# A fused attention and two-MLP kernel: seventeen weight units of the second MLP converted ahead, four raw buffers, and the x blocks in shared room

## The chip, the core and the metric

The kernel runs on one core of a Trainium2 chip. TensorE (PE) multiplies, VectorE (DVE), ScalarE (ACT) and GpSimd (POOL) work on what lies in SBUF and PSUM, and SyncE (SP) issues every DMA here. Each engine takes its own instructions in the order in which they stand in its queue, and waits on semaphores for the others. The metric is the device time in microseconds (us) of one execution of the whole program.

## What is computed

Attention with normalised q and k, a first MLP that is a product of two linear maps followed by two more, and a second MLP, which this change is about:

```python
def _moe2_ref(x, w_in, w_out):
    h = x @ w_in                          # 1792x768 @ 768x2048
    relu6 = np.clip(h + 3.0, 0.0, 6.0)
    g = h * relu6 / 6.0
    return (g @ w_out).astype(np.float32) # 1792x2048 @ 2048x768
```

The weights of both MLPs come in as 64-bit floats; q, k, v and all results are 32-bit.

## The kernel before

**Precision.** A product of 32-bit values is made of three matmuls (`mm3`, L80 to L83): each operand is split into a rounded part (hi) and the difference (lo), and hi·hi (L81), hi·lo (L82) and lo·hi (L83) are added up in PSUM.

**Weight units of the second MLP.** `win` and `wo2` are cut into 16 units each of 128 x 768, numbered 0 to 31: unit 2m is the part of `win` for step m, unit 2m+1 the part of `wo2` for step m. A unit goes through four stations. `load_w` (L818) brings its 64-bit words into a raw buffer `wr`, of which there are two. `conv_w` (L822) makes 32-bit floats of them with `convert` (L130): two ACT instructions (L137, L138) and two DVE instructions (L140, then L143, which writes the unit's tile `wf`). After that the raw buffer is free, and `conv_w(q)` issues the load of unit q+2 into it. `wf` stays in SBUF for the whole of the second MLP. Whenever a step uses the unit, `split` (L832) makes hi of it on ACT (L834) and lo on POOL (L835), as `wis` (from `win`) or `wos` (from `wo2`), each with two buffers.

**Steps and blocks.** The tokens are cut into four blocks of 448 columns, the block computed last by the first MLP goes first. Each block b runs through 16 steps m. Step m computes h (18 matmuls into one of two PSUM banks of tag `s`), then makes g of it: `u` on ACT (L906), `u` on DVE (L907), g hi on ACT (L910), g lo, the last difference, on DVE (L911). The second product of step m, `l4_part` (18 matmuls into six banks `acc`), is written behind h of step m+1, so TensorE has the h of the next step to do while g is made. At the end of a block the six results are copied out of `acc` (L867 to L870) and stored, and the next block's x is split into `x2h` (L810 to L813).

**What comes ahead.** The first 13 units (`NA = 13`, L797) are converted while the first MLP's last block still runs (L841 to L853), one at every third turn of the loop that also feeds the first MLP. The other units are converted in block 0: `conv_w` of units 2m+4 and 2m+5 is written at the head of step m, ahead of that step's splits (L878 to L881). The blocks of x and the results have eight tiles `xx` of 448 columns of their own (`x2tile`, L807), and x of block 1 is loaded at step 2 of block 0 (L882).

**What sets the order.** The code is written in this order, but a list scheduler places the instructions: within the data's constraints an engine's queue can differ from the written order, as the rows further down show. `tc.issue_after` keeps what is inside it behind a given instruction.

Of the kernel before, what the change touches and what calls it, by code (L numbers as in the profile page):

```python
# [12 lines left out]
F32 = mybir.dt.float32  # L13
# [4 lines left out]
AF = mybir.ActivationFunctionType  # L18
# [5 lines left out]
B, H, S, D = 4, 12, 448, 64  # L24
HP = H // 2
NP = B * HP
P = 128
# [3 lines left out]
DM = H * D  # L31
# [4 lines left out]
M2 = F2 // P  # L36
# [11 lines left out]
def fused_kernel(ctx: ExitStack, tc: tile.TileContext, nat, qT, kT, vin, gq, gk,  # L48
                 w12, w3t, wo, win, wo2, outT):
    nc = tc.nc  # L50
# [19 lines left out]
    def fetch(pool, src, n, tag, bufs=2):  # L70

        if src.dtype == F32:
            r = pool.tile([P, n], F32, tag=tag, bufs=bufs, name=tag)
            dma(r, src)
        else:
            r = pool.tile([P, n, 2], I32, tag=tag, bufs=bufs, name=tag)
            dma(r, src.bitcast(I32).rearrange("p (n t) -> p n t", t=2))
        return r

    def mm3(ps, lh, ll, rh, rl, first, last):  # L80
        nc.tensor.matmul(ps, lh, rh, start=first, stop=False)  # L81
        nc.tensor.matmul(ps, lh, rl, start=False, stop=False)  # L82
        return nc.tensor.matmul(ps, ll, rh, start=False, stop=last)  # L83

    def bank(tag, name="bank"):
        return pp.tile([P, 512], F32, tag=tag, name=name)

    def dma(out, src):
        return nc.sync.dma_start(out, src)
# [40 lines left out]
    def convert(w, r):  # L130

        hi, lo = r[:, :, 1], r[:, :, 0]
        top = r.bitcast(U16).rearrange("p n (t s) -> p n t s", s=2)[:, :, 0, 1]
        f = hi.bitcast(F32)
        nc.scalar.activation(f, f, AF.Copy, scale=2.0 ** -112)  # L137
        nc.scalar.activation(lo, top, AF.Copy, scale=2.0 ** -13, bias=2.0 ** -14 - 0.5)  # L138
        yield 0.7
        nc.vector.scalar_tensor_tensor(out=lo, in0=hi, scalar=SIGN, in1=lo,  # L140
                                       op0=ALU.bitwise_and, op1=ALU.bitwise_or)
        yield 0.9
        nc.vector.scalar_tensor_tensor(out=w, in0=hi, scalar=3, in1=lo,  # L143
                                       op0=ALU.logical_shift_left, op1=ALU.bitwise_or)
        yield 0.9
# [648 lines left out]
        attention(ap, rate)  # L794


    NA = 13  # L797
    order = [B - 1] + list(range(B - 1))
    d1 = ExitStack()
    x2p = d1.enter_context(tc.tile_pool(name="x2", bufs=1, side="left", **RW))  # L800
    wap = d1.enter_context(tc.tile_pool(name="wfa", bufs=1, side="left", **RW))
    xh = [None] * KD
    x2r = {}
    wf, wr = {}, {}
    wpools = [wap]

    def x2tile():  # L807
        return x2p.tile([P, S], F32, tag="xx", bufs=8, name="xx")

    def splitx2(n, src):  # L810
        d = x2p.tile([P, 2, S], F32R, tag="x2h", bufs=KD, name="x2h")
        nc.scalar.activation(d[:, 0, :], src, AF.Copy)
        nc.vector.tensor_sub(d[:, 1, :], src, d[:, 0, :])  # L813
        xh[n] = d
# [2 lines left out]

    def load_w(q):  # L818
        if q < 2 * M2:
            wr[q] = fetch(wap, (win, wo2)[q % 2][q // 2], DM, "wr", bufs=2)  # L820

    def conv_w(q):  # L822
        r = wr.pop(q)
        wf[q] = wpools[-1].tile([P, DM], F32, name=f"wf{q}")
        if r.dtype == F32:
            nc.gpsimd.tensor_copy(wf[q], r)
        else:
            for _ in convert(wf[q].bitcast(I32), r):
                pass
        load_w(q + 2)  # L830

    def split(q, tag, pool=None):  # L832
        t = (pool or lp).tile([P, 2, DM], F32R, tag=tag, bufs=2 if pool is None else 1, name=tag)
        nc.scalar.activation(t[:, 0, :], wf[q], AF.Copy)  # L834
        nc.gpsimd.tensor_sub(t[:, 1, :], wf[q], t[:, 0, :])  # L835
        return t

    load_w(0)
    load_w(1)
    step, q = 0, 0  # L840
    while not state["done"] or any(k >= now[0] for k in tasks):  # L841
        now[0] += 1
        fill(2.0, 3.0)
        run_tasks()
        step += 1
        if step > 2 and q < NA and step % 3 == 0:
            conv_w(q)
            q += 1
            if q == 1:
                wnext = split(0, "w0", wap)  # L850
    while q < NA:
        conv_w(q)
        q += 1  # L853
# [5 lines left out]
    lp = d1.enter_context(tc.tile_pool(name="l3", bufs=2, side="right", **RW))  # L859

    def l4_part(n, t, m, g, w, acc):
        ns = slice(n * P, n * P + P)
        return mm3(acc[n][:, :S], w[:, 0, ns], w[:, 1, ns], g[:, 0, :], g[:, 1, :], m == 0, m == M2 - 1)

    def out(n, t, acc):
        o = x2tile()
        if n % 2:  # L867
            nc.vector.tensor_copy(o, acc[n][:, :S])
        else:
            nc.scalar.activation(o, acc[n][:, :S], AF.Copy)  # L870
        dma(outT[n * P : n * P + P, t * S : t * S + S], o)

    pend = None
    for b, t in enumerate(order):
        acc = None
        for m in range(M2):
            last = b == B - 1 and m == M2 - 1
            if b == 0:  # L878
                for q in (2 * m + 4, 2 * m + 5):
                    if NA <= q < 2 * M2:  # L880
                        conv_w(q)  # L881
            if m == 2 and b < B - 1:  # L882
                for n in range(KD):
                    x2r[n] = x2tile()
                    dma(x2r[n], x2d[order[b + 1], n])
            w = wnext
            if not last:
                wnext = split(2 * ((m + 1) % M2), "wis")
            wos = split(2 * m + 1, "wos")
            ps = bank("s", "h2")  # L890
            for k in range(KD):
                ks = slice(k * P, k * P + P)
                mm3(ps[:, :S], w[:, 0, ks], w[:, 1, ks], xh[k][:, 0, :], xh[k][:, 1, :],
                    k == 0, k == KD - 1)
            if m == M2 - 1 and b < B - 1:
                for k in range(KD):
                    splitx2(k, x2r[k])
            if pend is not None and not last:
                for n in range(KD):
                    l4_part(n, *pend)  # L900
                    if m == 0:
                        out(n, pend[0], pend[4])
            if acc is None:
                acc = [bank(TAGS[1 + n // 2], "acc") for n in range(KD)]
            u = lp.tile([P, S], F32, tag="u", bufs=2, name="u")
            nc.scalar.activation(u, ps[:, :S], AF.Relu, bias=half, scale=1.0 / 6.0)  # L906
            nc.vector.scalar_tensor_tensor(out=u, in0=u, scalar=1.0, in1=ps[:, :S],  # L907
                                           op0=ALU.min, op1=ALU.mult)
            g = lp.tile([P, 2, S], F32R, tag="g", bufs=2, name="g")
            nc.scalar.activation(g[:, 0, :], u, AF.Copy)  # L910
            nc.vector.tensor_sub(g[:, 1, :], u, g[:, 0, :])  # L911
            before, pend = pend, (t, m, g, wos, acc)
    mm = None
    for e in (before, pend):
# [52 lines left out]
```

## Time and profile before

| | us |
|---|---|
| median of 3 runs | 1238.3 (1236.92 to 1243.6) |
| the profiled execution, its own time | 1239.83 |
| its span, first to last instruction | 1238.1 |
| PE busy | 1168.1 (94%) |
| DVE busy | 751.1 (61%) |
| ACT busy | 727.8 (59%) |
| POOL busy | 463.9 (37%) |

Attention and most of the first MLP take the first 640 us or so. The first MLP's last block and the first conversions of second-MLP weights fill the stretch to 748 us, where its last matmul runs. Block 0 of the second MLP runs from there to about 886 us, and blocks 1 to 3 take 118.4 us each, up to a short tail. A TensorE that counts as busy isn't at its peak: its matmuls are pipelined, a matmul of 448 columns counts as about 0.37 us, and a new one starts about every 0.205 us in the undisturbed blocks. So the count of matmuls in a stretch tells more of it than the busy share.

### The profile page before, as it was taken

Reading aid. Unit: us, or ns where it says so; the run is one execution under the profiler, and the core shown is the slowest. Engines: PE = TensorE matmul, PEld = TensorE weight load, DVE = VectorE, ACT = ScalarE, POOL = GpSimd, SP = SyncE. Lnnn points to the kernel's source line nnn. Section 1 sums busy time; section 2 is a strip of 40 time slices with the busy share of each in tenths; the row PEclk is TensorE's granted clock in tenths of the full one; section 3 lists DMA queues with packets and bytes.
Section 4 is the critical chain, followed back from the end, with each engine's and each line's share of the span. In section 5 each row is a group of like instructions: output and inputs, shape, how many; then the busy total and the mean of one; then the engine's idle time right before and its main releaser. Section 6 shows DMA issues by size and latency. Waiting matters only on the chain.

```text
span 1238.1 us, 16937 instructions
## 1 busy us (share of the span) xinstructions
PE 1168.1 (94%) x5868; PEld 1024.0 (83%) x5868; DVE 751.1 (61%) x1474; ACT 727.8 (59%) x1401; POOL 463.9 (37%) x316
## 2 busy tenths in 40 slices
PE   3698998988899999999999999989999999999998
PEld 2457877777789999889998998779999999999997
DVE  6977988998767787667624436774433333343332
ACT  6887788888857677666534435664533443343332
POOL 3534234553522213221020005445545445455442
PEclk9798998998999999999999999999999999999999
DMA  7667666797987777764469963440200020001001
GB/s 277 204 215 237 193 184 205 247 291 260 307 299 239 224 238 224 244 224 174 145 253 410 342 236 127 154 153 1 89 1 1 1 90 1 1 1 45 1 1 45
DMA packets 64694, 203.73 MB, mean 165 GB/s; under 512 B 8544, under 2 KB 25440, under 8 KB 64608
## 3 DMA queue, kind: packets, MB, share of 16 engines
q1 hardware_dynamic: 64608, 202.65, 48.4%
q8 instruction: 46, 0.75, 0.2%
q14 instruction: 40, 0.33, 0.1%
HBM read 173.93 MB, written 28.68 MB: 164 GB/s over the span
## 4 chain that ended last, share of the span: by engine, by line
PE 62%; DMA 4%; DVE 4%; ACT 3%; issue 2%; POOL 0%; SPq 0%; ACTq 0%; POOLq 0%; DVEq 0%
PE bank L81 7%; PE bank L83 7%; PE bank L82 7%; PE acc L81 6%; PE acc L82 6%; PE acc L83 6%; PE h L81 5%; PE h L82 5%; PE h L83 5%; PE bank L587 2%; PE bank L561 1%; PE bank L562 1%; DVE wf L143 1%; PE bank L639 1%; PE bank L640 1%
## 5 line engine op out<-in xcount | busy, mean ns | idle before, releaser
L835 POOL TENSOR_TENSOR wis<-wf,wis 128x768 fp32r<-128x768 f32 x63 | 120.9, 1919 | 234.3 <-ACT wis L834 234.3
L907 DVE SCALAR_TENSOR_TENSOR u<-u,h 128x448 f32<-128x448 f32 x64 | 39.6, 619 | 212.3 <-ACT u L906 212.3
L835 POOL TENSOR_TENSOR wos<-wf,wos 128x768 fp32r<-128x768 f32 x64 | 119.0, 1860 | 98.1 <-ACT wos L834 98.1
L580 ACT ACTIVATE PP<-PP,mx 112x448 f32<-112x448 f32 x192 | 127.4, 665 | 38.9 <-DVE mx L575 34.3
L568 DVE CUSTOM_DVE_ANT_0 PP<-bank,rb,rq 112x448 f32<-112x448 f32 x192 | 129.3, 677 | 32.0 <-PE bank L562 25.2
L81 PE MATMUL bank<-xhl,ws 128*128 128x448 f32 x384 | 143.1, 373 | 3.7 <-ACT ws L287 2.2
L83 PE MATMUL bank<-xhl,ws 128*128 128x448 f32 x384 | 141.5, 369 | 3.7 <-POOL ws L289 3.7
L82 PE MATMUL acc<-g,wos 128*128 128x448 f32 x384 | 142.6, 371 | 2.3 <-DVE g L911 2.3
L83 PE MATMUL acc<-g,wos 128*128 128x448 f32 x384 | 141.9, 369 | 0.0
L82 PE MATMUL bank<-xhl,ws 128*128 128x448 f32 x384 | 141.2, 368 | 0.0
L81 PE MATMUL acc<-g,wos 128*128 128x448 f32 x384 | 138.8, 374 | 2.5 <-ACT g L910 2.5
L81 PE MATMUL h<-x2h,wis 128*128 128x448 f32 x378 | 139.2, 368 | 0.6 <-DVE u L907 0.6
L83 PE MATMUL h<-x2h,wis 128*128 128x448 f32 x378 | 137.7, 364 | 2.2 <-POOL wis L835 2.2
L82 PE MATMUL h<-x2h,wis 128*128 128x448 f32 x378 | 139.0, 368 | 0.0
L906 ACT ACTIVATE u<-h,half 128x448 f32<-128x448 f32 x64 | 40.6, 634 | 141.1 <-PE h L83 141.1
L911 DVE TENSOR_TENSOR g<-u,g 128x448 fp32r<-128x448 f32 x64 | 99.5, 1554 | 35.4 <-ACT g L910 35.4
L606 DVE TENSOR_TENSOR xl<-bank,xh 128x448 fp32r<-128x448 f32 x142 | 87.4, 617 | 30.0 <-ACT xh L596 28.3
L834 ACT ACTIVATE wos<-wf 128x768 fp32r<-128x768 f32 x64 | 54.0, 844 | 84.2 <-PE acc L83 84.0
L587 PEld LDWEIGHTS bank<-ident,PP 112*128 112x128 f32 x672 | 79.3, 143 | 28.0 <-issue 9.7
L596 ACT ACTIVATE xh<-bank 128x448 fp32r<-128x448 f32 (+1 forms) x156 | 83.1, 539 | 32.4 <-PE bank L587 30.8
L587 PE MATMUL bank<-ident,PP 112*128 112x112 f32 x672 | 96.0, 266 | 6.5 <-DVE xl L606 5.2
L561 PE MATMUL bank<-K,Q 128*112 128x448 f32 x192 | 77.1, 403 | 24.1 <-DVE mx L568 12.7
(128 smaller groups left out, 2755.7 us busy)
## 6 DMA issues: line engine op xcount, KB each, us to landing
ws<-w12d SPq DMA_DIRECT2D x48, 768.0 KB
ws<-wpd SPq DMA_DIRECT2D x32, 768.0 KB
raw<-in_w_dram SPq DMA_DIRECT2D x32, 384.0 KB
w12d<-ws SPq DMA_DIRECT2D x16, 768.0 KB
wr<-in_win_dram SPq DMA_DIRECT2D x16, 768.0 KB
wr<-in_wo_dram SPq DMA_DIRECT2D x16, 768.0 KB
qr<-in_qT_dram SPq DMA_DIRECT2D x24, 448.0 KB
kr<-in_kT_dram SPq DMA_DIRECT2D x24, 448.0 KB
```

What stands on the lines that cost most here:

```text
L81: nc.tensor.matmul(ps, lh, rh, start=first, stop=False)
L82: nc.tensor.matmul(ps, lh, rl, start=False, stop=False)
L83: return nc.tensor.matmul(ps, ll, rh, start=False, stop=last)
L561: nc.tensor.matmul(ps[:CP, :S], qs, k1[:, j, :], start=True, stop=False)
L568: anchors[8 * i + s].append(nc.vector.tensor_tensor_reduce(out=T["PP", i][:, c, sl], in0=ps[:CP, :S], in1=T["rb", i][:, sl], op0=ALU.mult, ...
L580: anchors[8 * i + s].append(nc.scalar.activation(v, v, AF.Exp, bias=T["m", i][:, 8 + s : 9 + s], accum_out=T["sum", i][:, s : s + 1]))
L587: nc.tensor.transpose(ps[:, c * CP : c * CP + CP], src[:, c, kb * P : kb * P + P], ident[:CP, :CP])
L596: nc.scalar.activation(hi, ps, AF.Copy)
L606: nc.vector.tensor_sub(lo, ps, hi)
L834: nc.scalar.activation(t[:, 0, :], wf[q], AF.Copy)
L835: nc.gpsimd.tensor_sub(t[:, 1, :], wf[q], t[:, 0, :])
L911: nc.vector.tensor_sub(g[:, 1, :], u, g[:, 0, :])
```

## The change

`NA` goes from 13 to 17. The eight tiles `xx` are gone: `x2tile` now takes a tile of the size of a raw weight buffer (tag `wr`, two buffers, or tag `w0`, one buffer, which also holds the split unit of step 0) and hands out three parts of 448 columns of it. Four raw buffers serve the units from 17 on: the two `wr`, one more `wr` in the pool `lp` on the other side of SBUF, and `w0` after step 0; `conv_w(q)` loads unit q+4 into the one that it frees. In block 0 the conversions of step m are kept behind both last instructions of the step before (`done`: g hi and g lo), and there are one or two of them: units up to 17 + (5m+5)//4 are done after step m. The x of block 1 is loaded at step 14 instead of step 2 (m == M2 - 2); later blocks keep step 2.

```diff
-    NA = 13
+    NA = 17
...
+    xx = [0, None]
+
     def x2tile():
-        return x2p.tile([P, S], F32, tag="xx", bufs=8, name="xx")
+
+        n = 2 * DM // S if win.dtype != F32 else DM // S
+        z = xx[0] % n
+        if z == 0:
+            tag, bufs = ("w0", 1) if xx[0] // n % 3 == 2 else ("wr", 2)
+            xx[1] = wap.tile([P, n * S + (2 * DM % S if n > 1 else DM % S)], F32, tag=tag, bufs=bufs, name=tag)
+        xx[0] += 1
+        return xx[1][:, z * S : z * S + S]
...
         if q < 2 * M2:
-            wr[q] = fetch(wap, (win, wo2)[q % 2][q // 2], DM, "wr", bufs=2)
+            pool, tag, n = (wap, "wr", 2)
+            if q >= NA + 2 and (q - NA) % 4 > 1:
+                pool, tag, n = (lp, "wr", 1) if (q - NA) % 4 == 2 else (wap, "w0", 1)
+            wr[q] = fetch(pool, (win, wo2)[q % 2][q // 2], DM, tag, bufs=n)
...
-        load_w(q + 2)
+        load_w(q + (2 if q < NA else 4))
...
-    pend = None
+    load_w(NA + 2)
+
+    pend, done = None, []
...
             if b == 0:
-                for q in (2 * m + 4, 2 * m + 5):
-                    if NA <= q < 2 * M2:
+                if m == 1:
+                    load_w(NA + 3)
+                with ExitStack() as es:
+                    for i in done:
+                        es.enter_context(tc.issue_after(i.ins))
+                    while q < min(2 * M2, max(NA + (5 * m + 5) // 4, 2 * m + 6)):
                         conv_w(q)
-            if m == 2 and b < B - 1:
+                        q += 1
+            if m == (2 if b else M2 - 2) and b < B - 1:
...
-            nc.scalar.activation(g[:, 0, :], u, AF.Copy)
-            nc.vector.tensor_sub(g[:, 1, :], u, g[:, 0, :])
+            done = [nc.scalar.activation(g[:, 0, :], u, AF.Copy),
+                    nc.vector.tensor_sub(g[:, 1, :], u, g[:, 0, :])]
```

How the queues move is shown at three places. In the rows, L137, L138, L140 and L143 are the four instructions of a conversion, `wfN` is unit N, and the lines of the changed code are 12 to 19 higher (L846 is the split's L834, L925 the `u` on ACT, L926 the `u` on DVE, L929 and L930 the two halves of g, L821 the split of x).

ACT in block 0, steps 3 and 4, before:

```order
L906 ACTIVATE u_8082<-h2_8045,half_75 128x448
L834 ACTIVATE wis_8095<-wf10_7760 128x768
L137 ACTIVATE wr_8275<-wr_8275 128x768
L138 ACTIVATE wr_8275<-wr_8275 128x768
L910 ACTIVATE g_8085<-u_8082 128x448
L834 ACTIVATE wos_8098<-wf9_7714 128x768
L137 ACTIVATE wr_8282<-wr_8282 128x768
L138 ACTIVATE wr_8282<-wr_8282 128x768
L906 ACTIVATE u_8138<-h2_8101,half_75 128x448
L834 ACTIVATE wis_8158<-wf12_7853 128x768
```

The same steps, now:

```order
L925 ACTIVATE u_8137<-h2_8100,half_75 128x448
L846 ACTIVATE wis_8150<-wf10_7760 128x768
L929 ACTIVATE g_8140<-u_8137 128x448
L137 ACTIVATE wr_7973<-wr_7973 128x768
L138 ACTIVATE wr_7973<-wr_7973 128x768
L846 ACTIVATE wos_8153<-wf9_7714 128x768
L925 ACTIVATE u_8193<-h2_8156,half_75 128x448
L846 ACTIVATE wis_8206<-wf12_7853 128x768
```

Before, a conversion stood between `u` and g and another in front of the next `u`; now one stands behind g, and `u`, the split and g follow each other.

DVE at the same steps, before:

```order
L907 SCALAR_TENSOR_TENSOR u_8082<-u_8082,h2_8045 128x448
L143 SCALAR_TENSOR_TENSOR wf19_8277<-wr_8219 128x768
L140 SCALAR_TENSOR_TENSOR wr_8275<-wr_8275 128x768
L911 TENSOR_TENSOR g_8085<-u_8082,g_8085 128x448
L143 SCALAR_TENSOR_TENSOR wf20_8333<-wr_8275 128x768
L140 SCALAR_TENSOR_TENSOR wr_8282<-wr_8282 128x768
L907 SCALAR_TENSOR_TENSOR u_8138<-u_8138,h2_8101 128x448
```

The same steps, now:

```order
L926 SCALAR_TENSOR_TENSOR u_8137<-u_8137,h2_8100 128x448
L930 TENSOR_TENSOR g_8140<-u_8137,g_8140 128x448
L140 SCALAR_TENSOR_TENSOR wr_7973<-wr_7973 128x768
L143 SCALAR_TENSOR_TENSOR wf22_8143<-wr_7973 128x768
L926 SCALAR_TENSOR_TENSOR u_8193<-u_8193,h2_8156 128x448
```

Here too the halves of conversions that stood between `u` and g, and ahead of the next `u`, have become one conversion behind g; it is of unit 22 where it was of 19 to 21.

ACT at the end of the first MLP, from the split of x's third or fourth part (of six) to the first splits of weights, before:

```order
L137 ACTIVATE wr_7858<-wr_7858 128x768
L138 ACTIVATE wr_7858<-wr_7858 128x768
L812 ACTIVATE x2h_7837<-bank_7783 128x448
L812 ACTIVATE x2h_7869<-bank_7818 128x448
L812 ACTIVATE x2h_7881<-bank_7846 128x448
L834 ACTIVATE wis_7892<-wf2_7370 128x768
L834 ACTIVATE wos_7895<-wf1_7320 128x768
```

The same place, now:

```order
L821 ACTIVATE x2h_7837<-bank_7783 128x448
L137 ACTIVATE wr_7858<-wr_7858 128x768
L138 ACTIVATE wr_7858<-wr_7858 128x768
L137 ACTIVATE wr_7889<-wr_7889 128x768
L138 ACTIVATE wr_7889<-wr_7889 128x768
L821 ACTIVATE x2h_7869<-bank_7818 128x448
L137 ACTIVATE wr_7896<-wr_7896 128x768
L138 ACTIVATE wr_7896<-wr_7896 128x768
L821 ACTIVATE x2h_7881<-bank_7846 128x448
L846 ACTIVATE wis_7929<-wf2_7370 128x768
L846 ACTIVATE wos_7932<-wf1_7320 128x768
```

Unit 14 (`wr_7858`) has moved behind x's fourth part, and the conversions of units 15 and 16 stand ahead of its fifth and sixth. Unit 17's stands behind four splits of weights and ahead of block 0's first `u`. So 18 conversions now stand ahead of that `u` on ACT, where there were 15.

## Rows read from the trace of the kernel before

**Rows 1.** Windows: start:end, length, busy us (count) by engine, TensorE clock, DMA share, GB/s.

```profile
748.00:886.60 138.60, 130.99 (x608) 115.25 (x607) 88.19 (x78) 79.34 (x114) 71.69 (x36) 0.98 0.30 105
886.60:1005.00 118.40, 118.40 (x577) 108.09 (x576) 43.60 (x41) 48.54 (x73) 59.16 (x32) 1.00 0.07 23
...
787.00:794.00 7.00, 5.49 (x18) 4.07 (x17) 6.56 (x6) 4.56 (x7) 4.03 (x3) 0.76 0.44 150
...
822.00:829.00 7.00, 5.20 (x17) 4.43 (x17) 4.39 (x5) 4.87 (x7) 3.69 (x2) 0.76 0.56 209
```

**Rows 2.** Waits of PE, 748 to 886.6 us: us in total, times, longest.

```profile
PE acc L81 <- ACT g L910: 2.5, 3, 1.3
PE acc L82 <- DVE g L911: 2.3, 4, 0.6
PE h L83 <- POOL wis L835: 2.2, 3, 0.9
PE h L81 <- DVE u L907: 0.6, 1, 0.6
```

**Rows 3.** Timeline of ACT, steps 3 and 4: start, duration, [idle before, releaser].

```profile
784.46 0.91 ACT L137 ACTIVATE wr<-wr 128x768 f32<-128x768 f32 x1 [3.19 <-DMA wr<-in_wo_dram]
...
786.05 0.62 ACT L906 ACTIVATE u<-h,half 128x448 f32<-128x448 f32 x1
```

**Rows 4.** Timeline of PE: the first wait of block 0.

```profile
751.34 0.47 PE L83 MATMUL h<-x2h,wis 128*128 128x448 f32 x1 [0.45 <-POOL wis L835]
```

**Rows 5.** Groups by line, 748 to 840 us: busy us, mean ns, idle before.

```profile
L143 DVE SCALAR_TENSOR_TENSOR wf<-wr 128x768 int32<-128x768 int32 x17 | 35.1, 2064 | 0.3
L140 DVE SCALAR_TENSOR_TENSOR wr<-wr 128x768 int32<-128x768 int32 x17 | 19.0, 1116 | 17.4 <-ACT wr L138 17.4
...
L137 ACT ACTIVATE wr<-wr 128x768 f32<-128x768 f32 x17 | 15.4, 906 | 20.7 <-DMA wr<-in_wo_dram 13.7 <-DMA wr<-in_win_dram 6.9
```

**Rows 6.** The same view for block 1, 886.6 to 1005 us.

```profile
L911 DVE TENSOR_TENSOR g<-u,g 128x448 fp32r<-128x448 f32 x16 | 27.6, 1723 | 9.6 <-ACT g L910 9.6
L907 DVE SCALAR_TENSOR_TENSOR u<-u,h 128x448 f32<-128x448 f32 x16 | 9.9, 620 | 63.3 <-ACT u L906 63.3
...
L835 POOL TENSOR_TENSOR wis<-wf,wis 128x768 fp32r<-128x768 f32 x16 | 29.8, 1860 | 38.6 <-ACT wis L834 38.6
```

**Rows 7.** Timelines of DVE and POOL in block 0.

```profile
757.84 2.60 DVE L143 SCALAR_TENSOR_TENSOR wf<-wr 128x768 int32<-128x768 int32 x1
...
773.01 0.96 DVE L143 SCALAR_TENSOR_TENSOR wf<-wr 128x768 int32<-128x768 int32 x1
...
770.37 2.60 DVE L140 SCALAR_TENSOR_TENSOR wr<-wr 128x768 int32<-128x768 int32 x1
...
757.40 2.23 POOL L835 TENSOR_TENSOR wis<-wf,wis 128x768 fp32r<-128x768 f32 x1
```

**Rows 8.** Waits of PE, 640 to 748 us.

```profile
PE bank L81 <- ACT bs L316: 1.4, 1, 1.4
```

**Rows 9.** Timelines of SP and ACT, first MLP's last block.

```profile
643.72 5.99 SPq L89 DMA_DIRECT2D xx<-x2d  x4
...
654.91 0.33 SPq L89 DMA_DIRECT2D wr<-in_wo_dram  x1
...
663.80 0.90 ACT L137 ACTIVATE wr<-wr 128x768 f32<-128x768 f32 x1 [2.17 <-DMA wr<-in_wo_dram]
```

**Rows 10.** Timelines of ACT and SP around the start of block 0.

```profile
737.36 0.55 ACT L812 ACTIVATE x2h<-bank 128x448 fp32r<-128x448 f32 x1 [2.08 <-PE bank L83]
...
748.09 0.55 ACT L812 ACTIVATE x2h<-bank 128x448 fp32r<-128x448 f32 x1 [4.41 <-PE bank L83]
...
751.47 0.63 ACT L906 ACTIVATE u<-h,half 128x448 f32<-128x448 f32 x1
...
760.52 0.33 SPq L89 DMA_DIRECT2D wr<-in_wo_dram  x1
...
764.68 0.91 ACT L137 ACTIVATE wr<-wr 128x768 f32<-128x768 f32 x1 [1.83 <-DMA wr<-in_wo_dram]
```

## The prediction, made before the changed kernel was run

> **What bounds the kernel now.** I read the busy time by stretch first. In blocks 1 and 2 of the second MLP TensorE runs without a gap: 577 matmuls in 118.40 us, one per 0.2052 us, and 118.40/16 = 7.40 us for a step [rows 1]. The stretch from 748 to 886.6 us, block 0 and the start of block 1, has 608 matmuls in 138.60 us. At the undisturbed pace they need 608 x 0.2052 = 124.8 us, so 13.8 us are lost there, and there alone after 748 us but for the tail.
>
> The waits of TensorE in that stretch come next. They sum to 7.6 us: 4.8 on the two halves of g, 2.2 on the lo half of `wis`, 0.6 on the `u` that frees a bank [rows 2]. A second part is the clock: 787 to 794 us ran at a mean granted 0.76, a mix of the 2.4 and 1.2 GHz levels, and did 18 matmuls in 5.49 busy us where 5.49/0.2052 = 27 fit. 822 to 829 us is the same with 17 in 5.20, where 25 fit [rows 1]. That is (9 + 8) x 0.2052 = 3.5 us, both times right after TensorE had stood waiting. The remaining 2.7 us I put to the restart behind each of the 11 waits.
>
> Then I ask who holds up g, `u` and `wis`. On ACT the first instruction of a conversion waited 20.7 us for raw weights in block 0 [rows 5], and whatever stands behind it waits too: at 784.46 us ACT had been idle 3.19 us for a load, and step 4's `u`, whose h was long done, came at 786.05 [rows 3]. On DVE the two merges of a unit take 2.06 and 1.12 us on average [rows 5], and they stand between `u` and g. So the loss comes from conversions that stand ahead of a step's own chain, and from loads that are issued only when one of two buffers comes free.
>
> **The change part by part.**
>
> *Order in block 0.* From step 3 on both queues read u, split, g, conversion. Counted from the end of h of step m: ACT's `u` 0.62 [rows 3], a split 0.7 (the four between 748.5 and 751.47 us [rows 10]), g hi 0.6 like `u`; DVE's `u` 0.62 and g lo 1.72 [rows 6]. g is complete by about 3.8 us, and `acc` of step m starts 7.4 us after the end of h, since acc of step m-1 and h of step m+1 lie between. The conversion takes 1.6 us on ACT (784.46 to 786.05 [rows 3]) and 3.2 on DVE, from about 3.6 to 7 us, and is over when the next `u` comes at 8. In total DVE needs 0.62 + 1.72 + 1.25 x 3.18 = 6.3 us of a step's 7.4. So a step with one conversion costs nothing; the cover is TensorE's own 7.4 us.
>
> *Steps 3, 7 and 11* convert two units. On ACT the second ends at 2.0 + 2 x 1.6 = 5.2 us, the split of `wos` at 5.9, its lo on POOL 1.86 later [rows 6], at 7.8, and the third matmul of `acc` asks for it at 7.8. If POOL has to stand behind a merge of 0.96 us [rows 7], it is late by up to 0.9. Between 0 and 0.9 I take 0.4 each: 1.2 us.
>
> *Four raw buffers.* A buffer is used again after 4/1.25 = 3.2 steps, 24 us, while a load takes 4.2 us from issue to ACT (760.52 to 764.68 [rows 10]). The 20.7 us of ACT waits should go. On SP, the load of unit 18 now stands behind that of 20, which waits until step 0 has used `w0`, at about 751.5 us; unit 18 then lands near 757 and is asked for behind g of step 0, at about 757. I count this as nothing.
>
> *Start of block 0.* The first wait of 0.45 us, on POOL's lo for step 1 [rows 4], stays: 0.5. Unit 17's conversion now stands ahead of the first `u` on ACT and moves it from 751.47 [rows 10] to 753.1. On DVE its first merge stands ahead of that `u`: 0.96 to 2.60 us [rows 7]. So the bank of step 0 comes free between 754.7 and 756.4, while TensorE is through h of step 1 at about 754.9 and wants that bank for step 2: 0 to 1.5 us, I take 1.0. The remaining loss of block 0 is 1.2 + 0.5 + 1.0 = 2.7 us, and 13.8 - 2.7 = 11.1 us are won, the two drops of the clock among them.
>
> *More conversions in the first MLP's tail.* On ACT three more stand ahead of the first `u`: 15, 16 and 17. Behind x's fourth part (737.36 [rows 10]) come unit 14 at 737.9, 15 at 739.6; the buffer of 14 is free after its DVE merges, at about 741.7, unit 16 lands at 746, and its conversion is done at 747.6, just ahead of x's last part at 748.09 [rows 10]. That fits with half a us to spare; for a merge in front of that part on DVE I charge 0.5 us.
>
> *x of block 1.* Its six loads leave the most crowded part: SP spent 5.99 us on four of them at 643.72, and the raw load issued at 654.91 reached ACT only at 663.80, where ACT sat idle 2.17 us with L316 behind it [rows 9]. TensorE lost 1.4 us to that L316, its one wait between 640 and 748 us [rows 8]. With 1.4 MB less ahead of that load I count the 1.4 us as won; the bounds are 0 and 1.4. At their new place the loads are wanted at step 15, some 25 us after the raw buffers are done with.
>
> *The sum*: 11.1 + 1.4 - 0.5 = 12.0 us. Against the profiled execution's 1239.83 us that is 1227.8; it lies 1.5 us above the median of the runs, 1238.3, and from that median I get 1226.3 us. If all is won, 13.8 + 1.4 = 15.2 us, it is 1223.1.
>
> **The rivals.**
>
> *Late at the junction.* The load that took 8.9 us (654.91 to 663.80 [rows 9]) is what the tail of the first MLP can do. If unit 16 lands that late, at 750.7 us, its conversion ends at 752.3, and x's last part comes 4.2 us later than at 748.09, with TensorE idle, one drop of the clock (1.8 us) and 1.5 us more for unit 17 behind it: 7.5 us, 1233.8 us, which is no change by the measure below. It decides as soon as loads take over 5 us after 740 us. Against it: block 0's loads land in 4.2 us, and the first MLP's own loads are over by then.
>
> *VectorE becomes the bound; the result is slower.* If the merges take 2.60 us each beside POOL [rows 7], DVE needs 0.62 + 1.72 + 1.25 x 5.2 = 8.84 us a step. Twelve steps then lose 1.44 us each, 17.3 us; with 1.5 us at the start and two drops of the clock (3.5) block 0 loses 22.3 instead of 13.8 us. Less the 1.4 us won and plus the 0.5: 7.6 us slower, 1245.9. It decides from (7.40 - 2.34)/1.25 = 4.05 us per unit on; the mean of before is 3.18 [rows 5]. Against it: a merge alone takes 0.96, and the one that took 2.60 ended at 760.44, 0.81 us after POOL's subtraction that ran from 757.40 to 759.63 [rows 7]. So it waited for the end of POOL's instruction, and POOL has only two of them, 2 x 1.86 us, in a step.
>
> The Trainium skill (SBUF — State Buffer, "Who interferes with whom") says the same as a rule: VectorE and GpSimd share one pair of ports as an exclusive lock, and the loser is blocked for the whole instruction. By that rule the bill is POOL's 3.7 us plus 1.25 x 1.92 us of merges, 6.1 of 7.4 us, which leaves room for g; by the stretched durations it is the 8.84 us above.
>
> *It doesn't do what it says*: conversions still wait for their raw weights, say because loads 19 and 20 hold up SP. Then block 0 keeps its loss but for three of 17 conversions, 13.8 x 3/17 = 2.4 us, and with the 1.4 us the time is 1234.5. Against it are the four buffers' 24 us.
>
> **How the numbers follow.** A measurement of this kernel can tell about 0.5% from no change, so faster means under 1232.1 us, slower over 1244.5. Chances: the forecast 0.69, with a range of its own from 1223 to 1231; late at the junction 0.13; no effect in block 0 0.07; VectorE as the bound 0.11. That makes 0.70 for faster (some of the second case ends below 1232), 0.19 for the same, 0.11 for slower. The range goes from 1222.5, all won and a little for the spread of the runs, to 1237, beyond the two middle cases; it leaves out VectorE's.
>
> **What would show it.** Right: 608 matmuls from the first MLP's end in about 127.5 us instead of 138.6, no window at 0.76, ACT's wait for raw weights in block 0 under 3 us, TensorE's waits on g gone, a first wait on the bank or on `wis` lo of 1 to 2 us, and no wait on L316 in the tail. Blocks 1 to 3 stay at 118.4 us each. Wrong: TensorE waiting for x's last part near 748 us, merges on DVE close to 2.6 us with `u` waiting behind them, or ACT's first conversion instruction still idle for its DMA.

## The result, and the profile after

The changed kernel takes 1225.92 us in the median of 5 runs (1225.57 to 1228.09). The kernel before takes 1238.3 beside it (1234.26 to 1243.6), and the ratio is 0.9895 with a 95% interval of 0.987 to 0.992. The prediction was 1226.3 us. The profiled execution after took 1225.79 us, its span is 1224.0. That is 14.0 us less than the profiled execution of before, while the medians differ by 12.4. The reason for this difference comes with the first table.

The windows of the kernel after, with the columns of [rows 1]: block 0 from the first MLP's last matmuls to the start of block 1, block 1, and the two stretches in which the clock had fallen before.

```profile
747.30:872.50 125.20, 123.63 (x601) 112.27 (x600) 87.82 (x75) 75.26 (x109) 72.74 (x36) 1.00 0.33 111
872.50:990.90 118.40, 118.40 (x578) 108.09 (x577) 43.58 (x41) 48.54 (x73) 59.13 (x32) 1.00 0.09 29
787.00:794.00 7.00, 7.00 (x36) 6.39 (x35) 5.55 (x5) 3.95 (x7) 3.29 (x3) 1.00 0.37 131
822.00:829.00 7.00, 7.00 (x36) 6.38 (x34) 6.29 (x6) 5.47 (x9) 4.08 (x2) 1.00 0.48 152
```

Block 1 takes 118.40 us, as before. Block 0 now needs 125.20 us for 601 matmuls, 1.6 us more than the 123.6 at which TensorE was busy. The two stretches at a granted 0.76 are at 1.00 and hold 36 matmuls instead of 18 and 17.

The waits of TensorE after, 746 to 880 us, answering [rows 2]:

```profile
PE h L83 <- POOL wis L847: 1.6, 2, 1.2
```

Nothing is left on either half of g or on `u`. Between 640 and 746 us there is no wait of TensorE at all, where [rows 8] had 1.4 us on L316.

Groups by line after, 747 to 836 us, answering [rows 5]:

```profile
L143 DVE SCALAR_TENSOR_TENSOR wf<-wr 128x768 int32<-128x768 int32 x13 | 25.4, 1957 | 0.3
L140 DVE SCALAR_TENSOR_TENSOR wr<-wr 128x768 int32<-128x768 int32 x12 | 15.0, 1254 | 4.8 <-ACT wr L138 4.8
L137 ACT ACTIVATE wr<-wr 128x768 f32<-128x768 f32 x12 | 10.8, 903 | 0.0
```

The merges cost about what they cost before (1957 and 1254 ns against 2064 and 1116), and ScalarE's waits for raw weights in block 0, 20.7 us before, are gone (0.0 ahead of L137). Three units go through the buffer `w0` and are counted apart.

**Three stages.** Three fixed points cut a profile into stages that can be compared: the start of attention's last matmul (L639), the start of the first MLP's last matmul (L83 into `bank`), and the end of the span. For the kernel before and then the kernel after, the rows of TensorE's timeline at these points:

```profile
630.20 0.36 PE L639 MATMUL bank<-xh,vo 128*128 128x448 f32 x1
...
747.68 0.37 PE L83 MATMUL bank<-abh,ws 128*128 128x448 f32 x1
```

```profile
630.10 0.36 PE L639 MATMUL bank<-xh,vo 128*128 128x448 f32 x1
...
745.75 0.36 PE L83 MATMUL bank<-abh,ws 128*128 128x448 f32 x1
```

So the first MLP's tail took 747.68 - 630.20 = 117.48 us and now takes 115.65, and the rest of the span took 1238.1 - 747.68 = 490.4 and now takes 478.2. The same subtraction for every kernel of this study (one profile each):

| kernel | attention ends | tail | rest | median of runs | ratio to before (95%) |
|---|---|---|---|---|---|
| before | 630.2 | 117.5 | 490.4 | 1238.3 | 1 |
| after | 630.1 | 115.65 | 478.2 | 1225.9 | 0.9895 (0.987 to 0.992) |
| e1, no order | 630.8 | 115.65 | 487.2 | 1235.5 | 0.9951 (0.9923 to 0.9979) |
| e2, two buffers | 631.7 | 115.65 | 479.0 | 1228.2 | 0.9889 (0.980 to 0.998) |
| e3, neither | 630.9 | 115.65 | 490.1 | 1239.1 | 0.9976 (0.9945 to 1.0008) |
| e4, 13 ahead | 631.7 | 115.65 | 477.0 | 1228.9 | 0.990 (0.9872 to 0.9928) |
| e5, x written late | 634.0 | 117.6 | 489.9 | 1242.7 | 1.0003 (0.9976 to 1.0031) |
| e5b, x held back | 629.7 | 116.6 | 490.2 | 1238.7 | 0.9984 (0.9967 to 1.000) |
| e6, before with order | 630.5 | 117.4 | 493.0 | 1243.6 | 1.0021 (1.0001 to 1.0041) |
| e7, no conversions | 634.8 | 116.1 | 478.3 | 1228.5 | 0.9903 (0.9868 to 0.9939) |
| e8, lo on VectorE | 631.9 | 115.65 | 478.2 | 1227.8 | 0.9897 (0.9875 to 0.9919) |
| e10, one more merge | 632.1 | 115.64 | 497.6 | 1244.6 | 1.0033 (1.0007 to 1.0059) |
| e10, three more | 635.5 | 115.65 | 504.6 | 1256.8 | 1.0137 (1.0117 to 1.0158) |
| e11, order and rate | 632.0 | 117.6 | 477.6 | 1228.1 | 0.9876 (0.9842 to 0.991) |

The first stage is code that no kernel here edits, and it varies by 5.7 us from profile to profile. The other two repeat far better: the tail to 0.01 us in eight of the kernels, the rest to 0.5 us between before and e5, whose edit moved nothing there. So the verdicts below go by stages, and a difference of half a us in the rest is not read as one; the change is worth 1.8 us in the tail and 12.2 in the rest. The ratio of each e-kernel is taken against runs of before made beside it, whose medians were 1240.6 to 1242.9 us.

### The profile page after: what moved, and what is told of

Read it like the earlier page. It is cut to its first block, busy times and chain, and to the rows that moved or that the text cites. A ratio compares the mean times of both kernels' runs of the same rounds, so it can differ in the third digit from the quotient of the medians.

```text
span 1224.0 us, 16942 instructions
## 1 busy us (share of the span) xinstructions
PE 1162.5 (95%) x5868; PEld 1023.3 (84%) x5868; DVE 754.0 (62%) x1474; ACT 727.5 (59%) x1401; POOL 465.5 (38%) x316
## 4 chain that ended last, share of the span: by engine, by line
PE 68%; ACT 3%; DMA 2%; DVE 1%; issue 1%; POOL 1%; SPq 0%; POOLq 0%; ACTq 0%; DVEq 0%
PE bank L81 7%; PE bank L83 7%; PE bank L82 7%; PE acc L83 6%; PE acc L82 6%; PE acc L81 6%; PE h L81 6%; PE h L82 6%; PE h L83 6%; PE bank L587 2%; PE bank L561 1%; PE bank L562 1%; PE bank L639 1%; PE bank L640 1%; DMA rsb<-rsd 1%; ACT PP L580 1%
## 5 line engine op out<-in xcount | busy, mean ns | idle before, releaser
L926 DVE SCALAR_TENSOR_TENSOR u<-u,h 128x448 f32<-128x448 f32 x64 | 39.6, 619 | 210.6 <-ACT u L925 210.6
L83 PE MATMUL bank<-xhl,ws 128*128 128x448 f32 x384 | 142.1, 370 | 4.6 <-POOL ws L289 4.6
L83 PE MATMUL acc<-g,wos 128*128 128x448 f32 x384 | 141.3, 368 | 0.0
L83 PE MATMUL h<-x2h,wis 128*128 128x448 f32 x378 | 137.5, 364 | 1.6 <-POOL wis L847 1.6
L925 ACT ACTIVATE u<-h,half 128x448 f32<-128x448 f32 x64 | 40.8, 637 | 158.0 <-PE h L83 158.0
L930 DVE TENSOR_TENSOR g<-u,g 128x448 fp32r<-128x448 f32 x64 | 103.9, 1623 | 37.4 <-ACT g L929 37.4
L846 ACT ACTIVATE wos<-wf 128x768 fp32r<-128x768 f32 x64 | 54.2, 847 | 86.0 <-PE acc L83 85.7
L587 PEld LDWEIGHTS bank<-ident,PP 112*128 112x128 f32 x672 | 78.6, 142 | 26.4 <-issue 8.6
L561 PE MATMUL bank<-K,Q 128*112 128x448 f32 x192 | 77.4, 404 | 23.8 <-DVE mx L568 12.7
```

Of the source, the lines that this page charges most:

```text
L561: nc.tensor.matmul(ps[:CP, :S], qs, k1[:, j, :], start=True, stop=False)
L587: nc.tensor.transpose(ps[:, c * CP : c * CP + CP], src[:, c, kb * P : kb * P + P], ident[:CP, :CP])
L930: nc.vector.tensor_sub(g[:, 1, :], u, g[:, 0, :])]
```

## The experiments

**Order, and buffers.** The first three kernels take the changed kernel apart. e1 lets the conversions go where the scheduler wants them; e2 keeps them behind the last difference and has two raw buffers instead of four; e3 does both.

In e1 and e3:

```diff
-                with ExitStack() as es:
-                    for i in done:
-                        es.enter_context(tc.issue_after(i.ins))
```

In e2 and e3:

```diff
-            pool, tag, n = (wap, "wr", 2)
-            if q >= NA + 2 and (q - NA) % 4 > 1:
-                pool, tag, n = (lp, "wr", 1) if (q - NA) % 4 == 2 else (wap, "w0", 1)
-            wr[q] = fetch(pool, (win, wo2)[q % 2][q // 2], DM, tag, bufs=n)
+            wr[q] = fetch(wap, (win, wo2)[q % 2][q // 2], DM, "wr", bufs=2)
...
-        load_w(q + (2 if q < NA else 4))
+        load_w(q + 2)
```

Expected of e1:

> The changed kernel with its four raw buffers and its 17 units ahead, but the conversions of a step no longer kept behind the last difference of the step before: they are free to stand between u and g again. Two theories of the 12 us that block 0 won. Order (mine): the loss came from conversions that stand in a step's chain, so a good part comes back: TensorE again waits on g, 3 us or more in block 0, and the span is 1228 to 1233 us. Buffers: the loss came from loads issued too late, so nothing comes back: ACT waits under 2 us for raw weights and the span is 1223.5 to 1225.5 us.

Expected of e2:

> The changed kernel with two raw buffers in place of four (each conversion loads the unit two further on), the conversions still kept behind the last difference, 17 units ahead. Order: two buffers turn a unit round in about 4.5 us and a step wants 1.25 units in 7.4 us, so the second pair of buffers is hardly used: span 1223.5 to 1226 us, ACT waits a few us for raw weights in the steps with two conversions, behind g, where nothing of the chain stands. Buffers: the waits of ACT for raw weights come back (10 us or more) and hold up the next u: TensorE waits 4 us or more in block 0, span 1229 to 1234 us.

Expected of e3:

> The changed kernel with neither the four buffers nor the order: what stays is 17 units ahead, the 1.25 units a step and the x of block 1 loaded late. If the lead and the lower rate of conversions alone had brought the gain, the span is 1224 to 1226 us. Order and buffers both say that most of block 0's loss is back: 1231 to 1236 us, with waits of ACT for raw weights over 10 us and TensorE's waits on g over 3 us; the first MLP's tail keeps its gain, without a wait on L316.

The waits of TensorE in block 0, first e1, then e2, then e3:

```profile
PE h L81 <- DVE u L923: 4.1, 1, 4.1
PE acc L82 <- DVE g L927: 1.7, 1, 1.7
PE h L83 <- POOL wis L847: 1.6, 2, 1.2
```

```profile
PE h L83 <- POOL wis L844: 1.6, 2, 1.2
PE acc L82 <- DVE g L923: 0.7, 1, 0.7
```

```profile
PE acc L81 <- ACT g L919: 3.2, 3, 1.6
PE acc L82 <- DVE g L920: 2.7, 2, 2.1
PE h L83 <- POOL wis L844: 2.5, 3, 1.2
PE h L81 <- DVE u L916: 0.4, 1, 0.4
```

In the rest of the span, e2 keeps all but 0.7 of the 12.2 us, e1 keeps 3.2 and e3 0.3. What the order does is plain in e1: its 4.1 us are one wait, at 763.83 us, for a `u` that ScalarE had done with at 756.09 and VectorE began at 763.16, behind four merges that had started at 753.63, 755.63, 758.35 and 760.69; the granted clock from 756 to 776 us was 0.83. The forecast of e1 had named g as the wait, which was 1.7 us and not 3. ScalarE waited 10.7 us for raw weights in block 0 of e2 (7.2 for `win`, 3.5 for `wo2`), and it cost next to nothing, since behind g nothing urgent stands behind that wait. So four buffers alone don't do it, and the order does, given the rate. They matter more when the order is missing: 490.1 with two, 487.2 with four.

**Is order alone enough?** e6 gives the kernel before that order and nothing else: two conversions in a step, thirteen ahead, two buffers.

```diff
-                for q in (2 * m + 4, 2 * m + 5):
-                    if NA <= q < 2 * M2:
-                        conv_w(q)
+                with ExitStack() as es:
+                    for i in done:
+                        es.enter_context(tc.issue_after(i.ins))
+                    for q in (2 * m + 4, 2 * m + 5):
+                        if NA <= q < 2 * M2:
+                            conv_w(q)
```

> The kernel before with one thing of the change: block 0's two conversions of a step are kept behind g hi and g lo of the step before. NA 13, two raw buffers and x's own tiles stay. Order theory: most of the 138.6 - 124.8 = 13.8 us of block 0 goes, less what two units a step (0.62 + 1.72 + 2 x 3.18 = 8.7 of 7.4 us on VectorE, for about nine steps) and two buffers give back: span 1228 to 1232, TensorE's wait on L316 stays. Buffer theory: the raw weights come as late as before, so block 0 keeps its loss, span 1236 to 1240.

It came out at 493.0 us for the rest, 2.6 worse than before. My order theory, 1228 to 1232, is refuted in this form. The waits of TensorE, then of ScalarE in block 0:

```profile
PE acc L82 <- DVE g L914: 8.8, 6, 2.8
PE acc L81 <- ACT g L913: 2.3, 4, 1.0
```

```profile
ACT wr L137 <- DMA wr<-in_win_dram: 11.4, 7, 2.4
ACT wr L137 <- DMA wr<-in_wo_dram: 9.1, 8, 2.1
```

This is what a buffer theory says too, so two causes were open: two units are too many for a step, or two buffers are too few. e11 tells them apart. It keeps the two buffers, x's own tiles and `NA` = 13, and changes e6's rate alone. The lower rate also begins earlier: 1.25 units a step from step 0 on, where e6 has two a step from step 4 on. Block 0's first conversion starts on ScalarE 5.6 us after the first MLP's last matmul in e11 (755.17) and 23.8 us after it in e6 (771.71). "Rate" stands for both here; no run separates them.

```diff
-                    for q in (2 * m + 4, 2 * m + 5):
-                        if NA <= q < 2 * M2:
-                            conv_w(q)
+                    while q < min(2 * M2, max(NA + (5 * m + 5) // 4, 2 * m + 6)):
+                        conv_w(q)
+                        q += 1
```

> The kernel before with two things of the change: block 0's conversions stand behind g hi and g lo of the step before, and there are one or two of them a step (one at most steps, so 1.25 on average) instead of two. NA 13, two raw buffers and x's own eight tiles stay. Order-and-rate theory (neither works alone, both together carry block 0's gain; buffers and lead are nearly nothing): from the first MLP's last matmul to block 1 it takes 126 to 129 us instead of 138.9, the stretch from attention's last matmul to the first MLP's last stays at 117.4, span 1226.5 to 1230. Buffer theory (two buffers starve block 0 as long as x has its own tiles): block 0 stays above 135 us, span 1236 or more.

The rest fell to 477.6 us, and TensorE's waits from 640 us on are these:

```profile
PE bank L81 <- ACT bs L316: 1.5, 1, 1.5
PE acc L82 <- DVE g L914: 0.5, 1, 0.5
PE h L83 <- POOL wis L835: 0.4, 1, 0.4
```

That is the whole gain of block 0 with neither four buffers nor seventeen units ahead. The four combinations in one place, by the rest of the span: neither order nor rate 490.4 (before), order alone 493.0 (e6), rate alone 490.1 (e3, which also has 17 ahead), both 477.6 (e11).

**Units ahead.** e4 is the changed kernel with `NA = 13`.

> The changed kernel with NA = 13 again, everything else as changed: 19 units are left for block 0, 1.6 a step instead of 1.25. Order theory (what counts is that a conversion stands behind the step's last difference): VectorE has 0.62 + 1.72 + 1.6 x 3.18 = 7.4 us of work in a step of 7.4 us, so a few steps run late; span 1224 to 1228 us. Lead theory (the four more units ahead carry a good part of the 14 us): block 0 gets a third or more of its loss back, span 1229 to 1232.

One number in that text is wrong: by the formula there are 1.25 units a step until step 11 and two in steps 12 and 13, not 1.6 throughout. The rest is 477.0 us, 1.2 below the changed kernel's. The lead theory falls: four more units ahead bring nothing, and they cost some 1.2 us, of which the start of block 0, further down, shows 1.0. The 1.2 is one profile against one, though over the 0.5 above. e4 is the fastest kernel here by its stages; its median is 3 us above the changed kernel's, since the attention stage varies by more than that, so I don't claim it as faster.

**The tail.** The prediction put the 1.4 us on L316 down to the loads of x for block 1. e5 writes these loads at step 14 in the kernel before.

```diff
-            if m == 2 and b < B - 1:
+            if m == (2 if b else M2 - 2) and b < B - 1:
```

> The kernel before with one edit: the x of block 1 is loaded at step 14 of block 0 instead of step 2. My account of the first MLP's tail: the raw load that held up L316 lands earlier, TensorE's wait of 1.4 us there goes, and the span is 1.4 to 2 us shorter, 1236.0 to 1236.8, block 0 as before (13 to 14 us lost). Rival: the wait has nothing to do with the x loads, the raw load still lands late behind the first MLP's own weights, and the span stays at 1238.

Its SyncE timeline shows that the edit moved nothing: the four loads that [rows 9] has at 643.72 come at 647.52, 13.5 us after attention's last matmul in both.

```profile
647.52 5.88 SPq L89 DMA_DIRECT2D xx<-x2d  x4
```

With tiles of their own the loads went out at the same place from either written step. So the written step alone doesn't move them. In the changed kernel, where they share room with raw weights, they go out in block 0:

```profile
820.79 7.03 SPq L89 DMA_DIRECT2D wr<-x2d  x6
```

That the shared room does this, because a raw buffer must be free first, is argued: shared room with the loads written at step 2 wasn't run. e5 tests nothing of the claim on the tail; e5b does, with the loads held behind the last raw weight load.

```diff
-                    dma(x2r[n], x2d[order[b + 1], n])
+                    with tc.issue_after(sp[0].ins): dma(x2r[n], x2d[order[b + 1], n])
```

Here `sp[0]` is the DMA written last, and the loads are written at step 14.

> The kernel before, with the six loads of x for block 1 kept behind the last raw weight load on SyncE's queue, so that they truly leave the first MLP's last block. x-load theory: the raw load that reached ScalarE at 663.80 us comes earlier, TensorE's 1.4 us wait on L316 goes, and the last matmul of the first MLP comes 1.4 to 2 us sooner; block 0 as before; span 1236 to 1237. Rival (that stretch is late for other reasons): the wait on L316 stays above 1 us and the span at 1238 or more.

The only wait of a matmul between 640 and 748 us was this one, and no matmul waits for L316 any more:

```profile
660.70 0.48 PE L81 MATMUL bank<-xhl,ws 128*128 128x448 f32 x1 [0.30 <-ACT bs L357]
```

The tail fell from 117.48 to 116.57 us, half of the 1.83. All kernels with x's own tiles issued early (before, e5, e6, e11) have 117.4 to 117.6; eight of the nine with shared room have 115.65. So the loads are a cause, as predicted, but only half is shown by moving them alone. The other half lies at the same spot. TensorE's weight loads still waited 0.7 us for L357 and 0.3 for L316 in e5b, about the 0.9 that is left, and on ScalarE L357 stands behind a conversion that waited for its raw load. That row in e5b, then the same one after:

```profile
658.54 0.89 ACT L137 ACTIVATE wr<-wr 128x768 f32<-128x768 f32 x1 [5.39 <-DMA wr<-in_win_dram]
```

```profile
656.62 0.89 ACT L137 ACTIVATE wr<-wr 128x768 f32<-128x768 f32 x1 [3.71 <-DMA wr<-in_win_dram]
```

Counted from attention's last matmul that is 28.8 us in e5b and 26.5 after, so the raw load still lands 2.3 us later there. Why it does stays open.

**The floor of block 0.** e7 leaves units 17 to 31 out.

```diff
-                    while q < min(2 * M2, max(NA + (5 * m + 5) // 4, 2 * m + 6)):
-                        conv_w(q)
+                    while q < 2 * M2:
+                        wf[q] = wf[q - 16]
                         q += 1
```

> The changed kernel in which units 17 to 31 are neither loaded nor converted; the units 1 to 15 stand in for them, so block 0 has no conversions at all (this leaves out part of the computation). It is the floor for block 0. If what is left there comes from the conversions, the span falls from 1224.0 to about 1222 and TensorE's waits on the lo half of wis go; if it comes from the start of block 0 alone (the first splits and POOL's lo), the span stays at 1222.5 to 1224 and the same waits of 1 to 1.6 us are there.

The rest took 478.3 us against 478.2, with one wait of 1.2 us on `wis` at the start. So the fifteen conversions of block 0 now cost nothing measurable, and what is left is its start. (The span of 1229.2 is due to attention, which ended at 634.8 us.)

**The start of block 0.** After, one row each of TensorE, POOL and DVE; then POOL's same instruction in e4:

```profile
749.96 0.47 PE L83 MATMUL h<-x2h,wis 128*128 128x448 f32 x1 [1.19 <-POOL wis L847]
```

```profile
747.51 2.39 POOL L847 TENSOR_TENSOR wis<-wf,wis 128x768 fp32r<-128x768 f32 x1 [94.58 <-ACT wis L846]
```

```profile
747.27 0.95 DVE L143 SCALAR_TENSOR_TENSOR wf<-wr 128x768 int32<-128x768 int32 x1
```

```profile
749.07 1.84 POOL L847 TENSOR_TENSOR wis<-wf,wis 128x768 fp32r<-128x768 f32 x1 [93.50 <-ACT wis L846]
```

In both kernels POOL starts 1.76 us after the start of the first MLP's last matmul (745.75 and 747.31). With 17 ahead the last merge of unit 16 is on DVE then, and POOL takes 2.39 us instead of 1.84. e4 waits 0.6 us there instead of 1.6. e8 tries another cure: the lo halves of the three splits after step 0's are made on VectorE.

```diff
-        nc.gpsimd.tensor_sub(t[:, 1, :], wf[q], t[:, 0, :])
+        first[0] += 1
+        (nc.vector if 2 <= first[0] <= 4 else nc.gpsimd).tensor_sub(t[:, 1, :], wf[q], t[:, 0, :])
```

> The changed kernel with the lo halves of three splits at the start of block 0 made on VectorE instead of POOL. Theory (TensorE's waits of 1.6 us in all on wis at the start come from POOL's lo, which takes over 2 us beside VectorE): the waits go, span 1222.4 to 1223. Rival: VectorE's queue is as late as POOL's there, and the merges behind it move by as much; the waits change their name (wis from DVE, or u) and the span stays at 1223.5 to 1225.

The waits of TensorE:

```profile
PE h L81 <- DVE u L929: 1.3, 1, 1.3
PE h L83 <- DVE wis L848: 0.4, 1, 0.4
```

The rival was right: the wait changed its name from `wis` to `u`, and the rest stayed at 478.2 us.

**How near is VectorE to being the bound?** The last pair repeats the first merge (L140, whose result doesn't change by it) once or three times (n) for every unit converted in block 0.

```diff
+                if k == 1 and q >= NA:
+                    for _ in range(n):
+                        nc.vector.scalar_tensor_tensor(out=r[:, :, 0], in0=r[:, :, 1], scalar=SIGN, in1=r[:, :, 0],
+                                                       op0=ALU.bitwise_and, op1=ALU.bitwise_or)
```

> The changed kernel with the first merge (L140) of each of block 0's conversions done twice, which adds about 1.1 us x 1.25 = 1.4 us of VectorE work to a step. Slack theory: VectorE has 6.3 of 7.4 us, so 1.1 us are free and about 0.3 us a step, 3 to 5 us in all, come out late: span 1224 to 1229. Bound theory (VectorE is at its limit already, since its merges stretch beside POOL): 1.4 us x 12 steps appear in full, span 1238 or more.

> The changed kernel with the first merge (L140) of each of block 0's conversions done four times: 3 x 1.1 x 1.25 = 4.1 us more VectorE work a step. Slack theory: 6.3 + 4.1 = 10.4 us in a step of 7.4 us, 3 us late in each of 12 steps, 36 us, span about 1260; the clock falls in the waits. If merges in a row take the 0.96 us seen for one alone, 2.6 us less a step's slack: 1.6 x 12 = 19 us, span about 1243. Below 1235 VectorE's share of the bound was overrated throughout.

One more merge costs 19.3 us in the rest (497.6), three cost 26.4. The slack theory, at most 5 us for one, is refuted. First a step with one unit of the kernel after on DVE, then a step of the kernel with one more merge (L929 there is `u`, L843 the repeated merge):

```profile
778.17 0.61 DVE L926 SCALAR_TENSOR_TENSOR u<-u,h 128x448 f32<-128x448 f32 x1
779.42 1.02 DVE L930 TENSOR_TENSOR g<-u,g 128x448 fp32r<-128x448 f32 x1 [0.65 <-ACT g L929]
781.01 0.96 DVE L140 SCALAR_TENSOR_TENSOR wr<-wr 128x768 int32<-128x768 int32 x1 [0.57 <-ACT wr L138]
782.00 2.48 DVE L143 SCALAR_TENSOR_TENSOR wf<-wr 128x768 int32<-128x768 int32 x1
784.49 0.62 DVE L926 SCALAR_TENSOR_TENSOR u<-u,h 128x448 f32<-128x448 f32 x1
```

```profile
788.50 0.61 DVE L929 SCALAR_TENSOR_TENSOR u<-u,h 128x448 f32<-128x448 f32 x1
789.75 0.62 DVE L933 TENSOR_TENSOR g<-u,g 128x448 fp32r<-128x448 f32 x1 [0.64 <-ACT g L932]
791.33 0.96 DVE L140 SCALAR_TENSOR_TENSOR wr<-wr 128x768 int32<-128x768 int32 x1 [0.96 <-ACT wr L138]
792.33 2.49 DVE L843 SCALAR_TENSOR_TENSOR wr<-wr 128x768 int32<-128x768 int32 x1
794.85 2.48 DVE L143 SCALAR_TENSOR_TENSOR wf<-wr 128x768 int32<-128x768 int32 x1
797.26 0.61 DVE L929 SCALAR_TENSOR_TENSOR u<-u,h 128x448 f32<-128x448 f32 x1
```

A one-unit step of VectorE, where it doesn't wait for the next `u`, takes 784.49 - 778.17 = 6.32 us, a two-unit step 8.30 (`u` at 791.89 and 800.19), so four steps take 3 x 6.32 + 8.30 = 27.3 of TensorE's 29.6 us. Of these, 0.65 + 0.57 us a step are gaps in which VectorE waits for ScalarE's g hi and L138. They count as idle, and yet they aren't free for work that must come after them. With the merge the step takes 8.76 us, 1.36 over TensorE's 7.40; four steps, one of them with two units, run from 788.50 to 825.36, 36.9 us, so 7.3 over TensorE's 29.6, and three times that is 21.8, near the 19.3 measured. With three merges I expected 36 us and got 26.4. VectorE had no such gaps left there (1.3 us idle before g in all, 20.00 busy of every 20 us from 780 to 840), which goes in this direction. The busy times give the sum: from the first MLP's last matmul to block 1 VectorE was busy for 132.64 us (751.10 to 904.20) against 89.10 in the kernel after (745.75 to 872.50). The 45 repeated merges thus added 43.5 us, 0.97 each and not 1.1; 17.2 of it went into time that had been idle, and 26.4 came out as time.

## Why the prediction came out right, step by step

**Block 0's loss.** The view that carried it, matmuls counted at the undisturbed pace, held: 13.8 us were there to win, and the rest of the span gave back 12.2. The prediction had 11.1. Its cause was right in that the conversions had stood ahead of a step's own chain; e1 and e2 show it, with e3 as the control. The second cause that it named, loads issued too late for two buffers, was a symptom: e2 and e11 have two buffers and lose 0.7 us or nothing. And the prediction, which counted on 1.25 units a step, didn't say that without this rate the order brings nothing (e6 against e11, 15.4 us). Both drops of the clock went with the waits. The 2.7 us that it put to restarts weren't tested: after, TensorE's 1.57 idle us go with a loss of 1.9 by the prediction's count (125.20 - 601 x 0.2052), some 0.15 for each of two waits, so eleven would make 1.7 (an estimate); the other 1.0 stays open.

**What was left in block 0.** The total, 2.7 us predicted, came out as 1.6, with its parts the wrong way round. The first wait on `wis` was put at 0.5 us "as before" and was 1.2 and 0.4, since the added conversions bring a merge beside POOL's first subtraction. The bank of step 0 was put at 1.0 and cost nothing: DVE's `u` ended at 753.06 (752.45 + 0.61), ahead of the 754.7 to 756.4 of the prediction, and TensorE has no wait on a bank. The steps with two units were put at 1.2 and cost nothing.

**The tail.** 1.4 us predicted, 1.83 measured. Its stated cause, x's loads, accounts for 0.9 in e5b. The rest goes with a raw load that lands 2.3 us later in e5b than after, for a reason that stays open. The change names step 14 as the loads' new place; by e5 a later written step alone doesn't move them.

**The junction.** 0.5 us predicted, nothing measured. Unit 16 landed by 743.80 and not at the 746 of the prediction, as the first of these rows of ScalarE after shows, and x's last part waited for TensorE alone:

```profile
743.80 0.89 ACT L137 ACTIVATE wr<-wr 128x768 f32<-128x768 f32 x1 [1.97 <-DMA wr<-in_win_dram]
744.59 0.88 ACT L138 ACTIVATE wr<-wr 128x768 int32<-128x768 uint16 x1
746.15 0.54 ACT L821 ACTIVATE x2h<-bank 128x448 fp32r<-128x448 f32 x1 [0.68 <-PE bank L83]
```

**The sum.** 12.0 us predicted; 14.0 measured between the two profiles, by 1.1 in block 0, 0.4 in the tail and 0.5 at the junction. Against the medians, 12.4. That the predicted 1226.3 lies so near 1225.92 is partly luck, since the attention stage moves a median by more than the difference.

**The rivals.** Late at the junction and no effect in block 0 didn't come. VectorE as the bound didn't come either, but it was nearer than the prediction's point for it. The prediction set the point at 4.05 us per unit by adding up busy times (6.3 of 7.4 us a step). The two merges after take 1.96 + 1.25 = 3.2 us per unit on average, and with the 29.6 - 27.3 = 2.3 us left over for five units, 0.46 each, the point is at some 3.7 (an estimate from these rows). One merge of 2.49 us more a unit is far beyond it.

## What to carry over

Work that isn't urgent belongs behind the last instruction of a step's own chain on each engine, and in portions that the engine can finish before the next step's chain begins: here neither the order nor the portion brought anything worth naming alone (two raw buffers in both), and together, with the portions begun at step 0, they brought all of block 0's 12 us. Before buying buffers for a load that is waited for, look at what stands behind the waiting instruction; 10.7 us of such waits cost 0.7 at most once nothing urgent did. An engine's slack is its step's length from chain to chain, with the gaps in which it waits for a partner, not the span less its busy time.

## What the hardware showed that I had not expected

**Merges and subtractions in alternation.** POOL's two rows in the step with one more merge, to be read with VectorE's rows of that step:

```profile
792.11 1.89 POOL L850 TENSOR_TENSOR wos<-wf,wos 128x768 fp32r<-128x768 f32 x1 [4.35 <-ACT wos L849]
793.96 2.56 POOL L850 TENSOR_TENSOR wis<-wf,wis 128x768 fp32r<-128x768 f32 x1
```

VectorE's merge starts at 792.33, while POOL is at work, and ends at 794.82, 0.82 us after POOL's first row (792.11 + 1.89 = 794.00). POOL's second ends at 796.52, 1.70 us after that merge, and VectorE's next merge ends at 797.33, 0.81 after that. In this step each instruction appears to run alone, in turn, and the wait for the other counts as its own duration. The Trainium skill (SBUF — State Buffer, "Who interferes with whom") has this as an exclusive lock on a shared pair of ports, and these rows agree. What I hadn't expected is that the two engines take turns here, so that each of two merges in a row pays for a POOL instruction.

The turns aren't strict in general, though. In the kernel with three more merges, POOL, then VectorE:

```profile
778.48 5.39 POOL L850 TENSOR_TENSOR wos<-wf,wos 128x768 fp32r<-128x768 f32 x1 [7.42 <-ACT wos L849]
```

```profile
781.22 0.95 DVE L843 SCALAR_TENSOR_TENSOR w<-w 128x768 int32<-128x768 int32 x1
782.08 0.61 DVE L929 SCALAR_TENSOR_TENSOR u<-u,h 128x448 f32<-128x448 f32 x1
```

From 777.74 to 782.17 VectorE ran five merges back to back at 0.95 us each while POOL's one instruction stretched to 5.39. It ended at 783.87, 1.70 us after the last of these merges, so POOL got its turn when VectorE went on to `u`. There the subtraction paid for the merges and not the other way round; what decides which engine goes first stays open.

**The attention stage carries the spread.** Over fourteen profiles attention's last matmul started between 629.72 and 635.45 us, in code that none of the kernels edits, while the first MLP's tail behind it repeated to 0.01 us in eight of them.
